# A small add and its place: row sums written to PSUM ahead of a reciprocal, in a kernel of attention and two mixture stages

## The chip, the cores and the metric

The program runs on one core of one Trainium2 chip. The metric is device time of one execution in microseconds (us), as the median of several runs; smaller is better. One further execution was profiled.

## The reference

Attention over 4 batches, 8 heads, 576 positions and 64 dimensions with a causal mask by blocks of 64, then a dense stage of three products with a maximum over them, then a routed stage in which each of 2304 tokens goes to two of eight experts. What bears on the change is the softmax:

```
scores = q @ k.T / sqrt(64), masked where block_i < block_j
scores = scores - max(scores, axis=-1)
attn = exp(scores)
attn = attn / (sum(attn, axis=-1) + 1e-9)
out = attn @ v
```

The outputs of all heads are put side by side into rows of 512, and go on as `x`:

```
h = max(x @ w1, x @ w2, x @ w3);  x = h @ w_out
logits -> top two experts and their weights per token
out[token] += weight * (relu(x @ w1[e]) @ w2[e])
```

## The kernel before, in words

**Jobs.** Attention is cut into 32 jobs of two heads of one batch each. A job is early or late: an early one has the query blocks 0 to 3 (256 rows), a late one the blocks 4 to 8. Jobs 0 to 3 are the early ones of the first batch, jobs 4 to 7 those of the second batch; from job 8 on early and late jobs of the other batches alternate in a written list (`JOBS`). There are 16 late jobs.

**A softmax in one job.** Scores go into a PSUM bank. VectorE takes the negated maximum, ScalarE the exponential with that bias, and the row sum falls out of the same instruction into the small SBUF tile `st`. Then VectorE adds 1e-9 to a few sums in place (128 partitions, 1, 2 or 4 columns), takes the reciprocal in place, and the block of probabilities is multiplied by it, row by row. TensorE then transposes it (against `ident`), an engine copies it from PSUM, and TensorE multiplies it with the values. In an early job the two halves of the scores (blocks 3 and 2, then 0 and 1) have a bank each (`e_scores`, `e_max`, `e_exp`), and there is one add and one reciprocal for all four sums (`e_sums`, lines 352 and 353), then four multiplications (`e_scale`), on VectorE (line 360) or ScalarE (line 362). In a late job the order is block 4, 8, 6, 7, 5; `scale` (lines 366, 367, 371) comes after 8 for 4 and 8, after 7 for 6 and 7, after 5 for 5.

**PSUM.** Scores of kind "s" turn round in two banks; the kind "t", in four banks, takes transposes, value products and all products of the dense stage. Block 8 of a late job has two banks of its own (`a2`). A bank's next user waits for the last instruction that touches its content.

**The opening stage.** The dense weights come as 64-bit words and are taken apart: VectorE shifts (lines 525 and 526), ScalarE converts (line 530), GpSimd adds (line 539); ScalarE and GpSimd then split them into a high and a low part (lines 575 and 573). Meanwhile TensorE does the scores of jobs 0 to 7, the first unit's hidden products (line 584), their maxima being taken by VectorE (line 594), turns and products for the gates (lines 548, 558), and the first unit's long output products (line 601). All of this is handed to a planner (`start`, class `Plan`): each operation has an engine, a cost in us written beside it, the operations it depends on, and the kind of bank that it takes and gives back. The planner runs a clock over these costs and always takes the ready operation with the longest path behind it; instructions are emitted in the order that comes out, and each engine works through its own in that order.

**The rest.** Behind the opening stage the loop over jobs 8 to 31 writes, step by step, the transposes of job j, the scores of job j+1 and a budget of the next unit's dense products (`gap`, `filler`); the framework orders the instructions of this part on each engine by a simulated timeline of its own. For the next late job VectorE and GpSimd prepare low parts of queries, keys and values (lines 278, 272, 287). After the loop come the last unit and the eight experts, with weights split by ScalarE and GpSimd (lines 179, 180).

Of the kernel before, what the change touches and what calls it, by code (L numbers as in the profile page):

```python
# [14 lines left out]
OP = mybir.AluOpType  # L15
# [40 lines left out]
class Plan:  # L56
# [5 lines left out]
    def add(self, engine, cost, emit, deps=(), prio=0.0, take=None, give=None, late=0.1):  # L62
        self.ops.append((engine, cost, emit, tuple(deps), prio, take, give, late))
        return len(self.ops) - 1
# [54 lines left out]
def tile_attention_moe_moe(ctx, tc, qT, kT, v, w1, w2, w3, w_out, gates, noise, e1, e2, out):  # L119
    nc = tc.nc  # L120
# [112 lines left out]
    def bank(kind="m"):  # L233
        n, c = TAGS[kind]
        return (psS if n == "s" else psT).tile([128, 512], F32, name=n, bufs=c)

    psA = []
    RAW, RV, QK, VV, ST, XP = {}, {}, {}, {}, {}, {}
# [51 lines left out]
    def scores(ps, j, i, k0, k1):  # L290
        Kh, Kl = QK[j]
        QH, QL = (x[:, i - 4] for x in QQ)
        nc.tensor.matmul(ps, QH, Kh[:, k0:k1], start=True, stop=False)
        nc.tensor.matmul(ps, QL, Kh[:, k0:k1], start=False, stop=False)
        nc.tensor.matmul(ps, QH, Kl[:, k0:k1], start=False, stop=True)

    def exps(st, c, src, dst):
        ax = AX.XY if len(src.shape) == 3 else AX.X
        nc.vector.tensor_reduce(st[:, 0, c:c + 1], src, axis=ax, op=OP.max, negate=True)
        nc.scalar.activation(dst, src, AF.Exp, bias=st[:, 0, c:c + 1], scale=1.0, accum_out=st[:, 1, c:c + 1])  # L300

    def new_stats(j):
        if j not in ST:
            ST[j] = att.tile([128, 2, 5], F32, name="st", bufs=4)
        return ST[j]

    def s_block(j, i, c):
        st = new_stats(j)
        if i == 8:
            ps = psA[0].tile([128, 2, 512], F32, name="a2")  # L310
            for r in range(2):
                scores(ps[:, r, 0:288], j, i, 288 * r, 288 * r + 288)
            exps(st, c, ps[:, :, 0:288], PL[8][:, :576].rearrange("p (a b) -> p a b", a=2))
            return
        ps = bank("s")[:, :64 * i + 64]
        scores(ps, j, i, 0, 64 * i + 64)
        exps(st, c, ps, PL[i][:, :64 * i + 64])

# [5 lines left out]
    EPS = {}  # L324

    def e_scores(j, h, kind="s"):
        q, k = early_set(j)[:2]
        ps = EPS[j, h] = bank(kind)
        for x, i in zip((0, 256), EB[h]):
            nc.tensor.matmul(ps[:, x:x + 64 * i + 64], q[:, i], k[:, :64 * i + 64], start=True, stop=True)  # L330

    def e_max(j, h):
        st, ps = new_stats(j), EPS[j, h]
        for a, (x, i) in enumerate(zip((0, 256), EB[h])):
            nc.vector.tensor_reduce(ps[:, 448 + a:449 + a], ps[:, x:x + 64 * i + 64], axis=AX.X, op=OP.max, negate=True)
        nc.vector.tensor_scalar(st[:, 0, 2 * h:2 * h + 2], ps[:, 448:450], 0.125, None, op0=OP.mult)

    def e_exp(j, h):
        st, ps, p = ST[j], EPS[j, h], early_set(j)[3]
        for x, i in zip((0, 256), EB[h]):  # L340
            n, c = 64 * i + 64, EC[i]
            nc.scalar.activation(p[:, POFF[i]:POFF[i] + n], ps[:, x:x + n], AF.Exp, bias=st[:, 0, c:c + 1],
                                 scale=0.125, accum_out=st[:, 1, c:c + 1])
# [4 lines left out]
        e_exp(j, h)  # L348

    def e_sums(j):  # L350
        st = ST[j][:, 1, 0:4]
        nc.vector.tensor_scalar(st, st, 1.0e-9, None, op0=OP.add)
        nc.vector.reciprocal(st, st)

    def e_scale(j, on):
        for i, c in EC.items():
            P = early_set(j)[3][:, POFF[i]:POFF[i] + 64 * i + 64]
            x = ST[j][:, 1, c:c + 1]
            if on != "ACT":
                (nc.vector if on == "DVE" else nc.gpsimd).tensor_scalar(P, P, x, None, op0=OP.mult)  # L360
            else:
                nc.scalar.activation(P, P, AF.Copy, scale=x)

    def scale(j, c0, blocks):
        st = ST[j][:, 1, c0:c0 + len(blocks)]
        nc.vector.tensor_scalar(st, st, 1.0e-9, None, op0=OP.add)
        nc.vector.reciprocal(st, st)
        for c, i in enumerate(blocks):
            s = ST[j][:, 1, c0 + c:c0 + c + 1]
            P = PL[i][:, :64 * i + 64]  # L370
            nc.vector.tensor_scalar(P, P, s, None, op0=OP.mult)
# [24 lines left out]
    def e_turn(j, key):  # L396
        p = early_set(j)[3]
        ps = EPS[j, "t", key] = bank("t")
        for a, i in enumerate(range(4) if key == 0 else (2, 3)):
            o = POFF[i] + 128 * key  # L400
            nc.tensor.transpose(ps[:, 128 * a:128 * a + 128], p[:, o:o + 128], ident)

    def e_copy(j, key, eng):
        n = 2 if key else 4
        dst = early_set(j)[4][:, :, 256 * key:256 * key + 64 * n].rearrange("p h (i c) -> p i h c", c=64)
        src = EPS[j, "t", key][:, :128 * n].rearrange("p (i h c) -> p i h c", i=n, h=2)
        if eng == "ACT":
            nc.scalar.activation(dst, src, AF.Copy)
        else:
            nc.vector.tensor_copy(dst, src)  # L410
# [24 lines left out]
    def e_values(j, r):  # L435
        V, _, pt = early_set(j)[2:]
        if r == 0:
            EPS[j] = bank("t")[:, :256]
        p, m = EPS[j], slice(64 * r, 64 * r + 64)
        nc.tensor.matmul(p[m], V[:, r, 0:64], pt[:, r, 0:256], start=True, stop=False)  # L440
        nc.tensor.matmul(p[m, 128:256], V[:, r, 64:128], pt[:, r, 256:384], start=False, stop=True)

    def e_out(j):
        late, b, g = JOBS[j]
        x = new_x(2 * b, g)
        if b == 0:
            nc.scalar.activation(x, EPS[j], AF.Copy)
        else:
            nc.scalar.activation(x[:, 0], EPS[j], AF.Copy)
            nc.vector.tensor_sub(x[:, 1], EPS[j], plain(x[:, 0]))  # L450
# [172 lines left out]
    def start():  # L623
        pl = Plan({"s": 2, "t": 4})
        add = pl.add
# [28 lines left out]
        def job(j):  # L654
            old = next((x for x in range(j) if SETS[x] == SETS[j]), None)
            p = j + 0.5 if j < 4 else 25.0 + j
            sb = "t" if j in (1, 3) else "s"
            ex = []
            for h in (0, 1):
                s = ES[j, h] = add("PE", (0.76, 0.34)[h], lambda h=h: e_scores(j, h, sb), [LQ[j], LV[j]], p, take=sb)  # L660
                m = add("DVE", (0.7, 0.45)[h], lambda h=h: e_max(j, h), [s], p)
                ex.append(add("ACT", (0.9, 0.7)[h], lambda h=h: e_exp(j, h), [m] + ([ET[old]] if old is not None else []),
                              p, give=sb))
            r = add("DVE", 0.2, lambda: e_sums(j), ex, p)
            sc = "ACT" if j in (0, 4, 6) else "DVE"
            c = add(sc, 1.1 if sc == "DVE" else 1.35, lambda: e_scale(j, sc), [r], p)
            cp = []
            for key in (0, 1):
                ET[j] = add("PE", (0.46, 0.25)[key], lambda key=key: e_turn(j, key), [c], p, take="t")
                cp.append(add("ACT", (0.55, 0.4)[key], lambda key=key: e_copy(j, key, "ACT"),  # L670
                              [ET[j]] + ([EV[old]] if old is not None else []), p, give="t"))
            v = add("PE", 0.66, lambda: e_values(j, 0), cp + [LV[j]], p, take="t")
            v = EV[j] = add("PE", 0.66, lambda: e_values(j, 1), [v], p)
            EX[j] = add("ACT", 0.35 if j < 4 else 0.8, lambda: e_out(j), [v], p, give="t")
# [7 lines left out]
        for j in range(4):  # L682
            job(j)
# [45 lines left out]
        for g in range(3):  # L729
            cs = []  # L730
            for c in (0, 1):
                a = add("PE", 0.5, lambda g=g, c=c: gate_turn(g, c), [AD[18 + 2 * g], AD[19 + 2 * g]] + cs, 60.0, take="t")
                cs.append(add("ACT", 0.65, lambda g=g, c=c: gate_copy(g, c), [a] + ([done_g] if done_g else []), 45.0,
                              give="t"))
# [228 lines left out]
    def score_steps(j):  # L963
        if j >= NJ:
            return []
        if LATE[j]:
            return [lambda: s_block(j, 4, 0), lambda: (s_block(j, 8, 1), scale(j, 0, (4, 8))),
                    lambda: s_block(j, 6, 2), lambda: (s_block(j, 7, 3), scale(j, 2, (6, 7))),
                    lambda: (s_block(j, 5, 4), scale(j, 4, (5,)))]
        return [lambda: s_early(j, 0), lambda: (s_early(j, 1), e_sums(j), e_scale(j, "ACT"))]  # L970
# [93 lines left out]
    def bank2():  # L1064
        turn[0] ^= 1
        if turn[0]:
            return ps2.tile([128, 512], F32, name="b")
        return psT.tile([128, 512], F32, name="t", bufs=4)
# [150 lines left out]
    ps = bank2()  # L1219
# [77 lines left out]
    with tc.If(full > 0):  # L1297
# [10 lines left out]
        with tc.For_i(0, E) as e:  # L1308
# [4 lines left out]
            with tc.For_i(0, NT) as t:  # L1313
# [6 lines left out]
                ps = ps3.tile([128, 4, 128], F32, name="pa")  # L1320
# [66 lines left out]
```

## Time and profile before

| | us |
|---|---|
| median of 3 runs | 1029.79 |
| lowest and highest | 1027.38 and 1373.50 |
| the profiled execution | 1033.76 |
| its span from first to last instruction | 1032.0 |
| TensorE busy | 994.0 (96%) |
| VectorE busy | 495.6 (48%) |
| GpSimd busy | 457.2 (44%) |
| ScalarE busy | 418.3 (41%) |

The mean granted clock of TensorE over the span is 0.986 of full speed. In the profile the engines are PE (TensorE), PEld (its weight loads), DVE (VectorE), ACT (ScalarE), POOL (GpSimd) and SP. A row of a timeline gives the start, the time that a merged group of like instructions took, the engine, the line of the kernel, the operation, what it writes and reads, the count, and in brackets the engine's idle time ahead of it with what ended it. A tile is named by what was allocated under that name, so jobs share names: in the opening stage `Ph` holds probabilities of jobs 1, 2, 4 and 5, `Pl` of jobs 3 and 6, `pe` of jobs 0, 7 and 8, and scores stand as `s` or `t`.

### The profile page before, as it was taken

To read this page: it belongs to the slowest core of one execution; us is meant where nothing else is said; L and a number is where in the kernel's file an instruction comes from. 1 tells how busy PE (TensorE), PEld (TensorE's weight loads), DVE (VectorE), ACT (ScalarE), POOL (GpSimd) and SP (SyncE) were. 2 spreads that over 40 slices of the span, in tenths; PEclk is the share of its full clock that TensorE was granted. 3 is DMA by queue.
4 is the path that set the end of the run, shared out by engine and by line. 5 is a ranking of instruction groups with operands and counts; after the bars stand their busy time and mean duration, and the time that the engine had idled before them with its cause. 6 is when DMAs were issued, how large, how long until landed. Compare 5 with 4: busy or idle time off the path is not lost. (4 is left out here: it accounts for less than half of the span.)

```text
span 1032.0 us, 17334 instructions
## 1 busy us (share of the span) xinstructions
PE 994.0 (96%) x6557; PEld 903.8 (88%) x6557; DVE 495.6 (48%) x1328; ACT 418.3 (41%) x997; POOL 457.2 (44%) x381
## 2 busy tenths in 40 slices
PE   8979999999999999998999999999999999999997
PEld 5857899999999998898999979789898989888895
DVE  6883647866688857866237412222222222132221
ACT  5566446655456626545114332323141413242210
POOL 2776131331325232341224478765565648474302
PEclk9988999999999999999999999999999999999999
DMA  8921314312121211111202357563444435342201
GB/s 261 301 89 40 129 33 135 98 51 62 39 62 45 70 35 54 52 51 36 76 22 72 104 186 210 154 199 115 150 145 141 163 102 174 123 144 101 69 12 56
DMA packets 76262, 107.30 MB, mean 104 GB/s; under 512 B 23672, under 2 KB 48248, under 8 KB 76176
## 3 DMA queue, kind: packets, MB, share of 16 engines
q1 hardware_dynamic: 63408, 75.97, 23.9%
q0 software_dynamic: 10592, 29.41, 8.7%
q8 instruction: 52, 0.85, 0.3%
q10 hardware_dynamic: 2176, 0.79, 0.3%
q14 instruction: 34, 0.28, 0.1%
HBM read 86.66 MB, written 20.53 MB: 104 GB/s over the span
## 5 line engine op out<-in xcount | busy, mean ns | idle before, releaser
L180 POOL TENSOR_TENSOR w<-rw,w 128x1536 fp32r<-128x1536 f32 (+1 forms) x45 | 141.2, 3142 | 76.6 <-ACT w L179 62.5
L179 ACT ACTIVATE w<-rw 128x1536 fp32r<-128x1536 f32 (+1 forms) x45 | 60.3, 1343 | 114.5 <-DMA rw<-in_e 62.7
L1117 PE MATMUL b<-xh,w 128*128 128x384 f32 (+7 forms) x272 | 86.9, 321 | 0.9 <-ACT xh L1107 0.9
L1118 PE MATMUL b<-xl,w 128*128 128x384 f32 (+7 forms) x272 | 87.1, 320 | 0.1
L1119 PE MATMUL b<-xh,w 128*128 128x384 f32 (+7 forms) x272 | 87.0, 320 | 0.0
L762 PE MATMUL t<-xB,w 128*128 128x256 f32 x288 | 82.4, 287 | 1.6 <-DVE hm L769 0.9
L762 PE MATMUL t<-xA,w 128*128 128x256 f32 x288 | 82.2, 285 | 1.1 <-DVE hm L769 0.9
L763 PE MATMUL t<-xA,w 128*128 128x256 f32 x288 | 81.8, 284 | 1.0 <-DVE xA L450 1.0
L763 PE MATMUL t<-xB,w 128*128 128x256 f32 x288 | 82.3, 286 | 0.0
L764 PE MATMUL t<-xB,w 128*128 128x256 f32 x288 | 81.9, 285 | 0.0
L764 PE MATMUL t<-xA,w 128*128 128x256 f32 x288 | 81.5, 283 | 0.0
L777 POOL TENSOR_TENSOR hl<-hm,hh 128x512 fp32r<-128x512 f32 x21 | 27.7, 1321 | 114.8 <-ACT hh L776 113.8
L1166 POOL DMA_INDIRECT out_rows<-y,isc x40 | 40.6, 1014 | 79.5 <-DVE y L1165 72.6
L1122 DVE SCALAR_TENSOR_TENSOR ht<-b,ht 128x384 fp32r<-128x384 f32 (+6 forms) x56 | 29.1, 520 | 95.8 <-ACT ht L1121 95.8
L1161 PE MATMUL b<-w,ht 128*128 128x512 f32 (+1 forms) x168 | 67.4, 401 | 2.3 <-ACT ht L1121 2.3
L1165 DVE SCALAR_TENSOR_TENSOR y<-b,idt,prev 128x512 f32<-128x512 f32 (+1 forms) x24 | 18.0, 750 | 104.2 <-PE b L1163 76.3
L1119 PE MATMUL t<-xh,w 128*128 128x256 f32 x240 | 67.4, 281 | 0.0
L1118 PE MATMUL t<-xl,w 128*128 128x256 f32 x240 | 67.3, 281 | 0.0
L1117 PE MATMUL t<-xh,w 128*128 128x256 f32 x240 | 67.0, 281 | 0.0
L1163 PE MATMUL b<-w,ht 128*128 128x512 f32 (+1 forms) x168 | 66.7, 397 | 0.0
L1162 PE MATMUL b<-w,ht 128*128 128x512 f32 (+1 forms) x168 | 66.5, 396 | 0.0
L379 DVE TENSOR_TENSOR Pl<-t,Ph 128x512 fp32r<-128x512 f32 (+2 forms) x96 | 54.3, 572 | 20.3 <-ACT Ph L378 16.6
(388 smaller groups left out, 3019.1 us busy)
## 6 DMA issues: line engine op xcount, KB each, us to landing
rw<-in_e SPq DMA_DIRECT2D x32, 768.0 KB, 4.5
w<-in_w SPq DMA_DIRECT2D x18, 512.0 KB, 7.2
rw<-in_e SPq DMA_DIRECT2D x16, 512.0 KB, 3.7
rv<-in_v SPq DMA_DIRECT2D x16, 320.0 KB, 3.4
rk<-in_kT SPq DMA_DIRECT2D x16, 288.0 KB, 3.0
x2d<-x SPq DMA_DIRECT2D x18, 256.0 KB, 2.0
out_rows<-x SPq DMA_DIRECT2D x9, 512.0 KB, 3.1
w<-in_w_out SPq DMA_DIRECT2D x6, 512.0 KB, 6.7
```

What stands on the lines that cost most here:

```text
L179: nc.scalar.activation(t[:, 0, :c], r[:, :c], AF.Copy)
L180: nc.gpsimd.tensor_sub(t[:, 1, :c], r[:, :c], plain(t[:, 0, :c]))
L379: nc.vector.tensor_sub(dl, src, plain(dh))
L762: nc.tensor.matmul(ps[:, j], wh, x[:, 0], start=kt == 0, stop=False)
L763: nc.tensor.matmul(ps[:, j], wh, x[:, 1], start=False, stop=False)
L764: nc.tensor.matmul(ps[:, j], wl, x[:, 0], start=False, stop=kt == 3)
L1117: nc.tensor.matmul(p, wt1(e, 0, kt, f), th[:, kt, c0:c1], start=kt == 0, stop=False)
L1118: nc.tensor.matmul(p, wt1(e, 0, kt, f), tl[:, kt, c0:c1], start=False, stop=False)
L1119: nc.tensor.matmul(p, wt1(e, 1, kt, f), th[:, kt, c0:c1], start=False, stop=kt == 3)
L1161: nc.tensor.matmul(ps, a, wt2(e, 0, f), start=f == 0, stop=False)
L1162: nc.tensor.matmul(ps, a, wt2(e, 1, f), start=False, stop=False)
L1163: nc.tensor.matmul(ps, l, wt2(e, 0, f), start=False, stop=f == 7)
```

## The change

In `e_sums` and in `scale` the sum plus 1e-9 is no longer written back to `st` in SBUF. It goes into unused columns of a PSUM bank of scores: for an early job the bank of its second half (columns 456 to 459), for a late job the bank of the first block of the group (columns 500 and up of the bank of block 4, 6 or 5). The reciprocal reads it there and writes `st`. In the planner an early job's first half returns its bank after its exponentials, as before; the second half's bank is returned after the sums. The scaling of jobs 5 and 7 moves from VectorE to ScalarE in the opening stage, so that all of jobs 4 to 7 are scaled there.

```
+    SB = {}
 ...
     def s_block(j, i, c):
 ...
-        ps = bank("s")[:, :64 * i + 64]
+        SB[i] = bank("s")
+        ps = SB[i][:, :64 * i + 64]
 ...
     def e_sums(j):
-        st = ST[j][:, 1, 0:4]
-        nc.vector.tensor_scalar(st, st, 1.0e-9, None, op0=OP.add)
-        nc.vector.reciprocal(st, st)
+        st, z = ST[j][:, 1, 0:4], EPS[j, 1][:, 456:460]
+        nc.vector.tensor_scalar(z, st, 1.0e-9, None, op0=OP.add)
+        nc.vector.reciprocal(st, z)
 ...
     def scale(j, c0, blocks):
-        st = ST[j][:, 1, c0:c0 + len(blocks)]
-        nc.vector.tensor_scalar(st, st, 1.0e-9, None, op0=OP.add)
-        nc.vector.reciprocal(st, st)
+        st, z = ST[j][:, 1, c0:c0 + len(blocks)], SB[blocks[0]][:, 500:500 + len(blocks)]
+        nc.vector.tensor_scalar(z, st, 1.0e-9, None, op0=OP.add)
+        nc.vector.reciprocal(st, z)
 ...
     # in the planner, for each early job
-                              p, give=sb))
-            r = add("DVE", 0.2, lambda: e_sums(j), ex, p)
-            sc = "ACT" if j in (0, 4, 6) else "DVE"
+                              p, give=None if h else sb))
+            r = add("DVE", 0.2, lambda: e_sums(j), ex, p, give=sb)
+            sc = "DVE" if j in (1, 2, 3) else "ACT"
             c = add(sc, 1.1 if sc == "DVE" else 1.35, lambda: e_scale(j, sc), [r], p)
```

## Rows read from the trace of the kernel before

**Rows 1.** Busy us by stretch (instructions in brackets), granted clock, DMA share, GB/s.

```profile
core 0: us, PE busy (x) PEld busy (x) DVE busy (x) ACT busy (x) POOL busy (x), PEclk, DMA share, GB/s
52.00:62.00 10.00, 8.49 (x39) 6.72 (x38) 9.12 (x20) 7.58 (x20) 10.00 (x10) 1.00 0.56 204
...
68.70:73.70 5.00, 0.00 (x0) 0.00 (x0) 4.60 (x9) 2.05 (x9) 2.61 (x3) 0.78 0.00 0
73.70:83.10 9.40, 9.37 (x36) 8.72 (x37) 5.40 (x15) 6.59 (x20) 2.78 (x3) 0.50 0.13 31
83.10:97.10 14.00, 13.20 (x87) 10.86 (x86) 5.91 (x20) 11.22 (x33) 7.11 (x6) 0.93 0.15 41
97.10:130.00 32.90, 32.90 (x202) 25.95 (x202) 18.18 (x77) 14.91 (x42) 10.96 (x11) 1.00 0.34 111
130.00:482.00 352.00, 341.26 (x2671) 328.89 (x2669) 254.80 (x718) 194.90 (x528) 107.74 (x116) 1.00 0.20 59
```

**Rows 2.** Timeline of TensorE around the end of the opening stage.

```profile
66.80 1.89 PE L584 MATMUL t<-hl,w 128*128 128x256 f32 x8
73.73 1.22 PE L330 MATMUL s<-kve,qe 128*128 128x64 f32 x4 [5.03 <-ACT Pl L342]
...
97.12 4.45 PE L601 MATMUL t<-xB,hh 128*128 128x512 f32 x10
```

**Rows 3.** Timeline of ScalarE in the same stretch.

```profile
71.65 1.38 ACT L362 ACTIVATE Ph<-Ph,st 128x256 f32<-128x256 f32 x4 [5.37 <-DVE st L353]
72.94 0.29 ACT L342 ACTIVATE Pl<-s,st 128x64 f32<-128x64 f32 x1
...
73.48 0.19 ACT L342 ACTIVATION_READ_ACCUMULATOR Pl<-s,st 128x1 f32 x1
```

**Rows 4.** Timeline of VectorE in the same stretch.

```profile
65.80 5.55 DVE L352 TENSOR_SCALAR st<-st 128x4 f32<-128x4 f32 x1 [0.94 <-ACT Ph L342]
```

**Rows 5.** Timeline of GpSimd in the same stretch and behind it.

```profile
64.01 3.72 POOL L573 TENSOR_TENSOR w<-w 128x512 fp32r<-128x512 f32 x3
67.68 0.62 POOL L229 MEMSET Qh<- 128x640 f32 x1
68.27 2.47 POOL L573 TENSOR_TENSOR w<-w 128x512 fp32r<-128x512 f32 x2
70.69 0.62 POOL L229 MEMSET Ql<- 128x640 f32 x1
80.32 4.04 POOL L573 TENSOR_TENSOR w<-w 128x512 fp32r<-128x512 f32 x3 [9.01 <-ACT w L575]
```

**Rows 6.** Whole run: single lines, ns least/median/most, first and last start.

```profile
L352 DVE TENSOR_SCALAR st<-st x16: 159/172/5547, 11.0 to 275.2; 128x4 f32<-128x4 f32 x16
...
L525 DVE TENSOR_SCALAR sh<-w x24: 674/695/714, 12.8 to 61.2; 128x512 int32<-128x512 int32 x24
...
L336 DVE TENSOR_SCALAR st<-s x28: 97/159/161, 8.0 to 273.2; 128x2 f32<-128x2 f32 x28
```

**Rows 7.** Timeline of VectorE some microseconds later.

```profile
80.03 0.48 DVE L278 SCALAR_TENSOR_TENSOR Ql<-rq,Qh 64x320 fp32r<-64x320 f32 x1
80.44 1.24 DVE L352 TENSOR_SCALAR st<-st 128x4 f32<-128x4 f32 x1
81.71 1.52 DVE L278 SCALAR_TENSOR_TENSOR Ql<-rq,Qh 64x320 fp32r<-64x320 f32 x1
```

**Rows 8.** Line 366 in the whole run: busy us, mean ns, idle time before.

```profile
L366 DVE TENSOR_SCALAR st<-st 128x2 f32<-128x2 f32 (+1 forms) x48 | 12.9, 268 | 4.3 <-ACT p L300 3.5 <-issue 0.3
```

**Rows 9.** Timelines: block 5's scores and line 367, first and last late job.

```profile
107.40 0.34 PE L293 MATMUL s<-Kh,Qh 128*128 128x384 f32 x1
...
111.27 0.17 DVE L367 RECIPROCAL st<-st 128x2 f32<-128x2 f32 x1
...
473.89 0.34 PE L293 MATMUL s<-Kh,Qh 128*128 128x384 f32 x1
...
475.16 0.16 DVE L367 RECIPROCAL st<-st 128x2 f32<-128x2 f32 x1
```

**Rows 10.** What TensorE waited for, 110 to 482 us: total, times, longest.

```profile
PE s L293 <- ACT p L300: 0.7, 1, 0.7
```

## The prediction

> **What bounds the kernel now.** The first view is the busy table by stretch [rows 1]. TensorE works 32.90 of 32.90 us in the stretch from 97.1 us and 341.26 of 352.00 us in the loop over the attention jobs, so there anything spent on VectorE, ScalarE or GpSimd is covered unless TensorE stands in line for it. [...]
>
> [...] TensorE's scores of job 7, second half, start at 73.73 after 5.03 us of waiting for the exponentials of job 6 [rows 2]. Those exponentials run from 72.94 to 73.67, behind job 4's scaling on ScalarE, which waited 5.37 us for VectorE's reciprocal [rows 3]. The reciprocal stands behind the add of 1e-9 to four numbers, which takes 5.55 us, from 65.80 to 71.35 [rows 4]. In that time GpSimd runs without a pause from 64.01 to 71.31 [rows 5]: the add ends when GpSimd has run dry. A tiny add from SBUF to SBUF is thus the head of a chain of four engines.
>
> The third view, all executions of single lines, shows that this is a matter of place and not of work [rows 6]. Line 352 takes 172 ns in the median, 5547 at most. Line 525 is the same operation, but from SBUF into PSUM: 24 times, 674 to 714 ns for 512 columns, never longer, though GpSimd was busy all 10.00 us from 52 to 62 [rows 1] and the last of them started at 61.2. The last view asks what the loop's banks allow; it comes below.
>
> **The change, part by part.** The sum is made against the profiled execution, 1033.76 us (span 1032.0 and 1.76 around it). The median of the runs shown is 1029.79, 3.97 lower; the third run, 1373.50, lies far from the other two and carries nothing here.
>
> *Sums into PSUM, early jobs.* Sixteen adds lose their SBUF output. By line 525 the add no longer waits. Its own price is unseen for 4 columns from SBUF into PSUM; its nearest rows are line 336, which crosses the other way with 2 columns in 159 ns, and line 525, 695 ns for 512 columns [rows 6]; between these ends I take 0.16, by the row with the like number of columns. The reciprocal that reads PSUM is unseen too; line 336 reads PSUM in 159 ns where the SBUF add takes 159 at least and 172 in the median, so I take no change. If the price of both is off by 0.02 us, that is 64 times 0.02 = 1.3 us of VectorE time either way, hidden by VectorE's idle time (254.80 busy of 352.00 in the loop, rows 1).
>
> [...]
>
> In the opening the gain is worked out thus. Undelayed, job 4's sums end at about 66.2, its scaling (1.38 us) at 67.7, job 6's exponentials (0.73 us) at 68.4, and its sums, which the next bank now waits for too, at 68.8. TensorE's last group before the hole ends at 68.69 [rows 2]. Upper bound: the whole 5.03 us, and with no idle time no low clock: the 9.37 us busy at 0.50 are worth 4.7, together 9.7. Lower bound: the low clock stays and ScalarE's added 2.76 us (two scalings of 1.38) fall into the place of the wait, 5.03 - 2.76 = 2.3. I size ScalarE: from 68.7 to 97.1 it is busy 2.05 + 6.59 + 11.22 = 19.9 us [rows 1], the change puts two more scalings of 1.38 on it, 22.6 in 28.4 us. If all of that must be done before TensorE's long products at 97.12, 5.8 us can be saved; if the conversions that ScalarE starts last there can follow later, up to the 9.7. I take 6.5, nearer to ScalarE's bound, because ScalarE is the fuller engine from 83.1 on (11.22 of 14.00). The bounds are 2.3 and 9.7.
>
> The other two stalls of this line in the opening are near 1 us. The one at 80.44 has a neighbour, line 278, with two SBUF inputs, that stalls as well [rows 7]; it stays. I count them at nothing, but if the order shifts they are up to 1 us each.
>
> [...] The add at 80.44 took 1.24 us and line 278 behind it 1.52, against 0.48 a moment before, while GpSimd was in a run of three instructions of 4.04 us [rows 5, 7], about one instruction each; the one at 65.80 waited through six. [...]
>
> *Scales of jobs 5 and 7 to ScalarE.* VectorE loses two groups of four, ScalarE gains 2.8 us, counted above. Nothing on VectorE that needs SBUF at both ends is then left near the hole to inherit its stall.
>
> *Banks held longer, early.* The second half's bank comes back after the reciprocal instead of after the exponential: the add and the reciprocal, about 0.35 us, plus VectorE's queue. Scores of job 5, second half, wait for job 4's sums, 66.2 instead of 65.82. That is inside the 6.5. The planner lays the stage out afresh with the new returns and costs, so neighbours may swap in any queue; the longest group that could slip ahead of the scores is line 584's of 1.89 us [rows 2], and it is inside the bounds too.
>
> *Late jobs.* 48 adds go into the first block's score bank. They carry 12.9 us where 48 times 0.159 would be 7.6, so 5.3 us of stall [rows 8], for which no instruction of TensorE waited; behind them stands the scaling, SBUF at both ends, which will wait in their place. Gain: nothing. But two new waits arise in each of the 16 late jobs. Two banks turn round for blocks 4, 6, 7, 5 (block 8 has its own). Block 7 reuses block 4's bank, which now is busy until the reciprocal for blocks 4 and 8; block 5 reuses block 6's, busy until the reciprocal for 6 and 7, and that lies behind block 7's exponential. In the first late job block 5's scores start at 107.40 and that reciprocal ends at 111.44, 4.0 us later; in the last 473.89 and 475.33, 1.4 later [rows 9]. Of the 32 places 16 start today before the release they would have to wait for, by 55 us together. Behind such a wait stands all of TensorE's queue. What covers it is that the order outside the planned stage is laid out by a simulated timeline, which puts other ready products first; the unit products fill the loop. Bounds: 0 and +55. I take +2, near the lower end, because today's bank waits of the same kind cost 0.7 us in the whole loop [rows 10] with the same ordering. If that cover fails, block 5's max, exponential and scaling, about 3 us, become the next late thing.
>
> Sum: 1033.76 - 6.5 + 2 = 1029.3 for an execution like the profiled one, and 1029.79 - 4.5 = **1025.3** for the median.
>
> **The rivals.** *Full gain:* ScalarE's extra work finds room, the clock stays up, the loop costs nothing: -9.7, about 1020. For it: ScalarE was idle 2.95 of 5.00 us in the hole. Against: 11.22 of 14.00 later. Chance 0.20.
>
> *The held bank decides (the slower side):* TensorE stands at block 5's scores (line 293) because the laid-out order expects the reciprocal earlier than it comes. Above 6.5 us in sum, 0.4 us for each of 16 jobs, the change is slower than before; a third of the 55 us gives +12, about 1042; half gives +21, about 1051. For it: lags of 1 to 8 us at half of the places. Against: rows 10. Chance 0.20, of which 0.07 above 2%.
>
> *The change does not do what it says:* the add still waits when its output is in PSUM, since its input stays in SBUF. Then 1030 to 1033, the early scores with the longer-held banks. Against it stands line 525, from SBUF as well. Chance 0.06.
>
> *Forecast,* saving 1 to 8 us: 0.50. The remaining 0.04 is for more than 2% saved, which would need a second hole to close (TensorE's idle time in the loop is 10.7 us).
>
> **How the numbers follow.** 2% is 20.6 us, about what a measurement of this kernel can tell from no change. Faster by that: 0.04. Slower: 0.07. Within: 0.89. The range reaches from beyond the full gain, with the 3 us by which runs shown differ, 1014, to the held bank at a quarter of its price, +14 against 6.5, 1038.
>
> **What would show it.** In the changed profile: the early add (line 352 before) at 0.16 to 0.2 us everywhere; no hole of 5 us near 69 us and a granted clock of 1.00 there; TensorE's first long product (line 601 before) some 6 us earlier than 97.12; ScalarE fuller before it. In the loop, waits of the late scores' matmuls (line 293 before) for VectorE's reciprocal, in sum 0 to 4 us. Wrong would be: a new hole in the opening with ScalarE at its end, or waits at block 5's scores above 6 us in sum.

## The result and the profile after

| kernel | median us | least to most | runs | ratio to before, 95% interval |
|---|---|---|---|---|
| before | 1028.74 | 1024.87 to 1373.5 | 12 | |
| after | 1035.98 | 1032.01 to 1040.4 | 12 | 1.0076 [1.0055, 1.0097] |

The change makes the kernel slower by 0.76%, some 8 us (the run of 1373.5 us, far above the others, is left out of the ratio). Forecast were 1025.3 us, a gain of 4.5; the time is inside the range and inside 2%, but on the other side. The prediction took 2% as about what can be told from no change; the interval here is 0.2% to either side, so the loss is clear. Lines behind 317 stand three lower in the new kernel: 352 became 355, 353 became 356, 366 and 367 became 369 and 370, 371 became 374.

The opening looks as the prediction said. First the busy table by stretch of the changed kernel, with the columns of [rows 1]:

```profile
core 0: us, PE busy (x) PEld busy (x) DVE busy (x) ACT busy (x) POOL busy (x), PEclk, DMA share, GB/s
68.70:73.70 5.00, 5.00 (x38) 4.76 (x38) 2.56 (x10) 4.95 (x18) 2.38 (x3) 1.00 0.29 68
73.70:83.10 9.40, 9.14 (x63) 6.99 (x62) 2.36 (x9) 9.04 (x28) 1.66 (x2) 1.00 0.16 41
83.10:97.10 14.00, 12.86 (x48) 8.33 (x46) 1.80 (x5) 7.92 (x20) 14.00 (x13) 0.76 0.19 54
```

TensorE now works 5.00 of 5.00 us where it stood still [rows 1], at a granted clock of 1.00. The low clock has moved rather than gone, though: 0.76 in the row from 83.10, where the trace has 6.8 us at 0.50 from 86.0 us on, behind a wait of 1.14 us. The timeline of the same kernel around that place (start, us, engine, line, operation, tiles) and all its executions of the early add (ns least, median, most; first and last start):

```profile
65.75 0.17 DVE L355 TENSOR_SCALAR s<-st 128x4 f32<-128x4 f32 x1 [0.93 <-ACT Ph L345]
67.23 1.89 PE L587 MATMUL t<-hl,w 128*128 128x256 f32 x8
68.96 0.61 PE L333 MATMUL s<-kve,qe 128*128 128x64 f32 x4
...
88.94 6.37 PE L604 MATMUL t<-xB,hh 128*128 128x512 f32 x10
```

```profile
L355 DVE TENSOR_SCALAR s<-st x14: 153/166/167, 10.3 to 274.3; 128x4 f32<-128x4 f32 x14
...
L355 DVE TENSOR_SCALAR t<-st x2: 151/153/155, 16.6 to 20.1; 128x4 f32<-128x4 f32 x2
```

The add that took 5.55 us [rows 4] takes 0.17, the most of all sixteen is 167 ns, job 7's scores follow the group before them without a gap, and the first long product starts at 88.94 where it started at 97.12 [rows 2]: 8.2 us earlier. And yet the last product of this execution starts 3.3 us later than in the one before the change (1027.9 against 1024.6). So 8 us are won at 90 us, and 11 are lost behind it. Two questions follow: was there a hole in the other executions of the kernel before, and what is lost behind the opening? The waits of TensorE in the changed kernel from 110 to 560 us (engine, tile, line, what it waited for: us in total, times, longest) begin:

```profile
PE t L377 <- DVE p L374: 3.4, 2, 3.2
PE t L377 <- DVE Pl L382: 2.4, 1, 2.4
PE t L443 <- ACT rt L877: 2.3, 1, 2.3
PE s L293 <- ACT p L300: 1.5, 3, 0.6
PE s L294 <- DVE Ql L278: 1.4, 1, 1.4
```

The wait that the prediction named, scores (line 293) for the late reciprocal (line 370), is not among them. The long waits are few: transposes of a late block for its scaling (line 374), early value products (line 443).

### The profile page after: what moved, and what is told of

The parts are those of the page before. It is cut to its first block, busy times and chain, and to the rows that moved or that the text cites. A ratio compares the mean times of both kernels' runs of the same rounds, so it can differ in the third digit from the quotient of the medians.

```text
span 1035.2 us, 17369 instructions
## 1 busy us (share of the span) xinstructions
PE 995.3 (96%) x6557; PEld 902.8 (87%) x6557; DVE 482.7 (47%) x1320; ACT 424.1 (41%) x1005; POOL 455.8 (44%) x381
## 5 line engine op out<-in xcount | busy, mean ns | idle before, releaser
L765 PE MATMUL t<-xA,w 128*128 128x256 f32 x288 | 83.3, 289 | 1.0 <-DVE hm L772 0.9
L766 PE MATMUL t<-xA,w 128*128 128x256 f32 x288 | 82.5, 286 | 0.0
L767 PE MATMUL t<-xA,w 128*128 128x256 f32 x288 | 82.4, 286 | 0.0
L272 POOL TENSOR_TENSOR Kl<-rk,Kh 128x576 fp32r<-128x576 f32 x16 | 23.3, 1458 | 100.4 <-ACT Kh L271 100.4
```

Of the source, the lines that this page charges most:

```text
L765: nc.tensor.matmul(ps[:, j], wh, x[:, 0], start=kt == 0, stop=False)
L766: nc.tensor.matmul(ps[:, j], wh, x[:, 1], start=False, stop=False)
L767: nc.tensor.matmul(ps[:, j], wl, x[:, 0], start=False, stop=kt == 3)
```

## The experiments

The theories in the expectations: **H**, the banks held until the reciprocal cost the time; **W**, arithmetic on PSUM itself costs it; **P**, the lines happen to be laid out in a worse order, without relation to banks; **U**, the hole near 70 us belongs to the one profiled execution, against **S**, it is in every one; **R**, chance. All ratios are to the kernel before on the same chip, as recorded; the quotient of two medians can differ from them by up to 0.2%.

### Each half alone

Early sums in PSUM, late ones as before:

```diff
-        st, z = ST[j][:, 1, c0:c0 + len(blocks)], SB[blocks[0]][:, 500:500 + len(blocks)]
-        nc.vector.tensor_scalar(z, st, 1.0e-9, None, op0=OP.add)
-        nc.vector.reciprocal(st, z)
+        st = ST[j][:, 1, c0:c0 + len(blocks)]
+        nc.vector.tensor_scalar(st, st, 1.0e-9, None, op0=OP.add)
+        nc.vector.reciprocal(st, st)
```

> The change without its late half: early sums in PSUM, scales of jobs 5 and 7 on ScalarE, the late jobs' add in place in SBUF as before. Theory H (the longer-held score banks of the late jobs cost the time): the opening's gain of 7.2 us (long products at 88.9 in place of 97.1) is kept to the end, ratio to before 0.992 to 0.996. Theory W (the add and the reciprocal through PSUM cost more by themselves): about the same as H here, a little less gain. Theory P (any edit makes the framework lay the loop out anew, and this layout happened to be worse): ratio anywhere from 0.99 to 1.01, without relation to the opening's gain.

Measured: 1028.22 us, ratio 0.9993 [0.9976, 1.0011]. The reverse, the kernel before with the late sums alone in the score banks (the `SB` lines and `scale` of the diff):

> The late half alone: late sums in the bank of the group's first block, everything of the early jobs as before. H: slower than before by 10 to 15 us, ratio 1.010 to 1.015, with the hole of 5 us at 69 us still there and the loss in the loop from 110 to 490 us. W: also slower. P: anywhere from 0.99 to 1.01.

Measured: 1030.83 us, 1.0024 [1.0008, 1.0040]. Neither half is the whole: -0.07% and +0.24% don't add up to +0.76%. The early half, for which the sum had 6.5 us, brings none that can be told from nothing. In us: -0.7 and +2.5 make +1.8, and both together cost 7.8, so 6 us (some 3 to either side, by the three intervals) appear only when both halves are there. The expectation for the late half, 10 to 15 us with the hole still there, missed in both: in its profile there is no hole, and the early add in SBUF at that place reads:

```profile
65.61 0.52 DVE L355 TENSOR_SCALAR st<-st 128x4 f32<-128x4 f32 x1 [0.94 <-ACT Ph L345]
```

### The late sums in another bank

The whole change, but the sums of blocks 4, 8, 6 and 7 go to spare columns of block 8's own two banks, which don't turn round with the score banks; block 5's go to block 5's bank.

```diff
-            ps = psA[0].tile([128, 2, 512], F32, name="a2")
+            ps = SB[8] = psA[0].tile([128, 2, 512], F32, name="a2")
...
-        st, z = ST[j][:, 1, c0:c0 + len(blocks)], SB[blocks[0]][:, 500:500 + len(blocks)]
+        st, z = ST[j][:, 1, c0:c0 + len(blocks)], (SB[5] if blocks[0] == 5 else SB[8][:, 0])[:, 500 - c0:500 - c0 + len(blocks)]
```

> The whole change, but the late sums of blocks 4 and 8 and of 6 and 7 go into spare columns of block 8's own banks, so that the two score banks come back after the exponentials as in the kernel before; block 5's sum stays in its bank. H: as fast as the early half alone, ratio 0.992 to 0.997. W (PSUM itself): as slow as the whole change, 1.005 to 1.010. P: anywhere from 0.99 to 1.01.

Measured: 1026.26 us, 0.9981 [0.9966, 0.9997]. The same arithmetic on PSUM, with the sums of blocks 4, 8, 6 and 7 in another bank, is not slow: W falls.

### A hold without the arithmetic, first try

The kernel with the early half alone, and a write into the score bank behind the late reciprocal:

```diff
+        nc.vector.memset(SB[blocks[0]][:, 500:501], 0.0)
```

> Early half as changed; the late add and reciprocal in SBUF as before, but a memset of one column in the bank of the group's first block follows the reciprocal, so the bank is held as long as in the change while no sum goes through PSUM. The 48 memsets cost some 0.1 us each on VectorE, off TensorE's path. H: as slow as the whole change, ratio 1.005 to 1.012. W: as fast as the early half alone, 0.992 to 0.997. P: anywhere from 0.99 to 1.01.

Measured: 1028.61 us, 1.0006 [0.9991, 1.0021]. This tested nothing: the write uses nothing that the reciprocal makes, and in the trace it ran ahead of it (at 163.5 us with the reciprocal at 165.7, at 242.1 with 246.9), so the bank was not held as long as in the change.

### Both kernels profiled again

No edit: the kernel before and the changed one, once more.

> The kernel before, unchanged, profiled once more. Theory U (the stall of 5.55 us and the hole of 5.03 us at 69 us belonged to the one profiled execution, which at 1033.76 us was 5 us above the median): here the add at 66 us takes under 2 us, TensorE has no hole near 69 us, the first long product starts near 89.5 as in the run with the late half alone, not at 97.1, and the span is 1026 to 1028. Theory S (the hole is in every execution, and something later gives its gain back): stall of 5 us and hole again, first long product near 97.

> The changed kernel, unchanged, profiled once more. Theory P (the order that the framework lays out for the loop of this kernel costs the time): the same waits of TensorE come back, 2.3 us at 177 behind the second product of an early job, 2.4 us at 411, 1.4 us at 424, and the low clock behind most of them; span 1031 to 1037. Rival R (chance of the one execution): other waits, or the same with less low clock, and a span near 1029.

The kernel before took 1025.41 us (span 1023.6), the changed one 1033.97 (span 1032.2). In the second execution of the kernel before, the busy table (columns as above) and the timeline show at the place of the hole:

```profile
68.70:73.70 5.00, 5.00 (x37) 4.55 (x36) 4.62 (x15) 4.83 (x19) 2.70 (x3) 1.00 0.23 57
73.70:83.10 9.40, 6.65 (x43) 4.98 (x42) 6.53 (x15) 6.38 (x20) 3.75 (x3) 1.00 0.18 46
```

```profile
66.08 0.52 DVE L352 TENSOR_SCALAR st<-st 128x4 f32<-128x4 f32 x1 [0.93 <-ACT Ph L342]
...
68.98 0.71 PE L330 MATMUL s<-kve,qe 128*128 128x64 f32 x4
...
64.08 3.72 POOL L573 TENSOR_TENSOR w<-w 128x512 fp32r<-128x512 f32 x3
67.74 0.63 POOL L229 MEMSET Qh<- 128x640 f32 x1
68.33 2.50 POOL L573 TENSOR_TENSOR w<-w 128x512 fp32r<-128x512 f32 x2
...
89.96 4.45 PE L601 MATMUL t<-xB,hh 128*128 128x512 f32 x10
```

The same add, beside the same GpSimd instructions at the same times within 0.3 us [rows 4, 5], takes 0.52 us and not 5.55; there is no hole of 5 us (the 2.75 us of idle time from 73.70 on are waits of 1.1 us or less), and the first long product starts at 89.96, not at 97.12. The kernel with the late half alone, whose early jobs are those of the kernel before, agrees (0.52 us, 89.51). U stands, S falls: one execution of three has the hole. That one, at 1033.76 us, lies above 87 of the 89 timed runs of the kernel before (the others are 1034.33 and 1373.5): it was no typical one, and its time alone was a hint.

The changed kernel's second execution has the long waits of its first again (2.60 us at 171, 2.43 at 405, 1.39 at 419, 3.22 at 482), so R falls. Against the second execution of the kernel before it shows where the loss is. A unit product is here a matmul of line 762 (765 in the changed kernel), the first of three lines with a unit's hidden products, 576 in all. First starts, us:

| | before, again | after, again |
|---|---|---|
| first long product | 89.96 | 87.48 |
| unit product 1 of 576 | 109.4 | 105.5 |
| unit product 83 | 180.8 | 180.6 |
| unit product 329 | 369.5 | 370.4 |
| unit product 370 | 418.3 | 423.4 |
| unit product 452 | 488.3 | 495.0 |
| unit product 576 | 542.5 | 549.1 |
| last expert product | 1015.8 | 1024.4 |

By the first unit product 3.9 us are won; 3.7 of them are lost again by 181 us, 1.1 more by 370, 4.2 between 370 and 423, 1.6 by 490 and 2.0 in the experts. But not all of the 3.9 is gain: the changed order has 509 matmuls ahead of the first unit product, the kernel before 520. The 11 others are scores and come behind it: unit products are drawn forward. The kernel with the late half alone has the same 509, and the early half alone has 520 and starts its first unit product at 110.0.

### Two tries at chance

The changed kernel with a write into the score bank behind the late reciprocal (this time it did follow it, since the bank's own sums are read there), and the changed kernel with the scales of jobs 5 and 7 on VectorE as before:

```diff
-        nc.vector.reciprocal(st, z)
+        nc.vector.reciprocal(st, z); nc.vector.memset(SB[blocks[0]][:, 504:505], 0.0)
```

```diff
-            sc = "DVE" if j in (1, 2, 3) else "ACT"
+            sc = "ACT" if j in (0, 4, 6) else "DVE"
```

> The whole change plus a memset of one unused column of the same bank behind each late reciprocal, some 0.1 us on VectorE 48 times, and the banks held that much longer. It does more work than the change everywhere and holds longer. Theory H (held banks) and theory W (PSUM itself): ratio to before 1.007 to 1.012, no better than the change. Theory P (the laid-out order): the memsets shift the simulated timeline, another order comes out, and the ratio lies with the other variants, 0.997 to 1.004.

> The whole change, but the scales of jobs 5 and 7 stay on VectorE. On TensorE its order differs from the change's in some places of the opening stage only; the loop's order is the same. Theory P: as slow as the change, 1.005 to 1.010, with the same waits at 177, 411 and 424 us. If the loss sits in the opening (two more scales on ScalarE, 1.4 us each): 0.998 to 1.004.

Measured: 1034.34 us, 1.0054 [1.0036, 1.0072], and 1034.73 us, 1.0070 [1.0050, 1.0089]. Both keep most of the loss, and both show the long waits of the changed kernel again (2.90 and 2.56 us at line 443 near 175 us, 3.96 and 3.23 at line 377 near 485). The first has the changed kernel's matmul (by tiles and shape) at 6221 of 6557 places in TensorE's order, so it says little against P; the second moves the scales of the opening alone, so the loss is not theirs.

### What held banks do, seen in the two traces

The two places with a long wait lie at the end of a unit's dense products, the work that fills TensorE between the jobs' steps. Timeline of the kernel before, again: last of those products (line 788), scores of block 6 (448 columns) and of block 5 (384), the reciprocal (367) and scaling (371) of the late sums, and the wait behind:

```profile
162.76 0.45 PE L293 MATMUL s<-Kh,Qh 128*128 128x448 f32 x1
165.87 0.29 PE L788 MATMUL t<-w,hl 128*128 128x264 f32 x1
172.93 0.83 PE L440 MATMUL t<-pte,kve 128*64 128x256 f32 x3 [0.24 <-DVE pte L410]
...
466.83 0.34 PE L293 MATMUL s<-Kh,Qh 128*128 128x384 f32 x1
468.11 0.16 DVE L367 RECIPROCAL st<-st 128x2 f32<-128x2 f32 x1
468.94 0.29 PE L788 MATMUL t<-w,hl 128*128 128x264 f32 x1
469.95 0.42 DVE L371 TENSOR_SCALAR p<-p,st 128x384 f32<-128x384 f32 x1
476.20 0.55 PE L374 MATMUL t<-ident,p 128*128 128x128 f32 x3 [2.61 <-DVE Pl L379]
```

And of the changed kernel, again (those products: line 791):

```profile
162.58 0.29 PE L791 MATMUL t<-w,hl 128*128 128x264 f32 x1
163.56 0.18 DVE L356 RECIPROCAL st<-s 128x4 f32<-128x4 f32 x1
166.07 0.45 PE L293 MATMUL s<-Kh,Qh 128*128 128x448 f32 x1
170.89 1.08 PE L443 MATMUL t<-pte,kve 128*64 128x256 f32 x2 [2.60 <-ACT rt L877]
...
473.74 0.28 PE L791 MATMUL t<-w,hl 128*128 128x264 f32 x1
474.71 0.17 DVE L370 RECIPROCAL st<-s 128x2 f32<-128x2 f32 x1
476.72 0.42 PE L293 MATMUL s<-Kh,Qh 128*128 128x384 f32 x1
481.58 0.41 DVE L374 TENSOR_SCALAR p<-p,st 128x384 f32<-128x384 f32 x1
482.14 0.87 PE L377 MATMUL t<-ident,p 128*128 128x128 f32 x3 [3.22 <-DVE p L374]
```

Read the last late job. Before, block 5's scores start 1.3 us ahead of the reciprocal for blocks 6 and 7, and 1.9 us of dense products still follow to cover block 5's softmax. After, they come 1.8 us behind that reciprocal, when the dense products are used up, and max, exponential and scaling of block 5 stand bare: 3.22 us, where 2.61 were paid before. At 163 us the same happens to block 6: before, its scores start 3.4 us ahead of the end of the last dense product (162.76 against 166.16), after, 3.2 behind it and 2.3 behind the early job's reciprocal, and the wait behind grows from 0.24 to 2.60.

Which bank is waited for is not quite what the prediction had. Another late job of the changed kernel, again, shows it:

```profile
317.48 0.69 ACT L300 ACTIVATE p<-s,st 128x512 f32<-128x512 f32 x1 [1.07 <-DVE st L299]
318.31 0.44 PE L293 MATMUL s<-Kh,Qh 128*128 128x384 f32 x1 [0.62 <-ACT p L300]
318.98 0.16 DVE L370 RECIPROCAL st<-s 128x2 f32<-128x2 f32 x1
```

Block 5's scores start here 0.14 us behind the end of block 7's exponential and ahead of the reciprocal for 6 and 7. Over the 16 late jobs of this trace they are ahead of that reciprocal in 5, and never ahead of block 7's exponential; in the kernel before, again, they are ahead of block 7's exponential in 11, and never ahead of block 6's. So block 5 does not wait for block 6's held bank: going by these starts, it gets block 7's instead, and its wait is for block 7's exponential. Block 7 does wait for block 4's held bank: behind the reciprocal for 4 and 8 in all 16 jobs, by 0.06 us at the least, where 5 were ahead of it before. The two banks are thus not handed out in strict turn.

Beside such waits stand stretches at the low clock; the busy table of the changed kernel, again, in three such stretches (columns as above):

```profile
170.80:174.20 3.40, 3.31 (x13) 2.58 (x14) 3.21 (x9) 1.87 (x5) 0.19 (x1) 0.50 0.96 295
406.30:413.10 6.80, 6.53 (x23) 5.89 (x23) 4.34 (x19) 1.27 (x4) 0.00 (x0) 0.50 0.00 0
481.40:488.20 6.80, 5.33 (x23) 4.99 (x23) 3.30 (x18) 0.49 (x1) 0.00 (x0) 0.50 0.15 39
```

From 110 to 560 us the stretches at 0.50 sum to 20.5 us there and to 10.2 in the kernel before, again; TensorE is idle for 14.7 against 12.3 us (in the two first executions: 17.1 and 3.4 us at 0.50, 15.6 and 12.7 idle). From the first to the last unit product the changed kernel takes 443.6 us and the kernel before 433.1. Of these 10.5 us, 3.5 are idle time (14.4 against 10.9) and an estimated 4.9 are half of the 9.7 us more that TensorE works at 0.50 (the four products of job 7's scores took 1.22 us at 0.50 [rows 1, 2], and 0.61 in the changed kernel at 1.00); most of the remaining 2.1 is the 11 matmuls that stood ahead of the first unit product before (1.5 us: with the time at 0.50 taken by half, TensorE is busy for 99.5 us ahead of it there and for 98.0 here).

### The true hold, and each hold alone

The kernel with the early half alone, late sums in SBUF, and a copy of the late reciprocals into the score bank, so that the bank is held until they are done, with no arithmetic on it:

```diff
-        nc.vector.reciprocal(st, st)
+        nc.vector.reciprocal(st, st); nc.vector.tensor_copy(SB[blocks[0]][:, 500:500 + len(blocks)], st)
```

> The whole change but with the late sums added and inverted in SBUF as before; after each late reciprocal VectorE copies its result (one to two values a partition, 0.06 to 0.2 us a piece) into a spare column of the score bank in which the change would have put the sums, so the bank is held until after the reciprocal without any arithmetic on it; the output is unchanged. Theory H (the held score banks of the late jobs, together with the early jobs' second banks, cost the time): slower than the kernel before, ratio 1.004 to 1.010, with the first unit product as early as in the changed kernel and a wait of TensorE of 2 us or more near 170 to 180 us. Theory W (the arithmetic on PSUM costs it) and theory P (the order that the lines happen to give): ratio 0.998 to 1.003, as with the early pairs alone.

Measured: 1034.4 us, 1.0043 [1.0026, 1.0060]. Holds without arithmetic in the late jobs bring more than half of the loss back, and the picture with it. TensorE's timeline of this kernel:

```profile
164.34 0.29 PE L791 MATMUL t<-w,hl 128*128 128x264 f32 x1
167.43 0.45 PE L293 MATMUL s<-Kh,Qh 128*128 128x448 f32 x1
169.89 0.50 PE L293 MATMUL s<-Kh,Qh 128*128 128x512 f32 x1 [0.28 <-DVE s L370]
173.95 1.08 PE L443 MATMUL t<-pte,kve 128*64 128x256 f32 x2 [3.09 <-issue]
...
478.73 0.42 PE L293 MATMUL s<-Kh,Qh 128*128 128x384 f32 x1
484.83 0.87 PE L377 MATMUL t<-ident,p 128*128 128x128 f32 x3 [4.02 <-DVE ex L909]
```

Here even the wait that the prediction named shows once, for 0.28 us, though for block 7 (512 columns). The copies add 7.7 us to VectorE over the run. The kernel at 1.0054, with 2.8 us of such writes, lost no more than the change, which speaks against the copies as the loss; they were not run without a hold.

Then the whole change with only blocks 4 and 8, or only 6 and 7, moved to block 8's banks (with the `SB[8]` line above):

```diff
+        ... (SB[8][:, 0] if blocks[0] == 4 else SB[blocks[0]])[:, 500 - c0:500 - c0 + len(blocks)]
```

> The whole change, but the sums of blocks 4 and 8 go to spare columns of block 8's own two banks; those of blocks 6 and 7 stay in block 6's score bank, as in the change. Theory H: if the bank of block 4, held across block 8's exponentials, is the one that costs, ratio 0.997 to 1.001; if it is the bank of block 6, 1.005 to 1.009; if each costs a part, 1.001 to 1.005. Theory P: anything between 0.998 and 1.008 without relation to the other kernel of this pair.

```diff
+        ... (SB[8][:, 0] if blocks[0] == 6 else SB[blocks[0]])[:, 500 - c0:500 - c0 + len(blocks)]
```

> The mirror of the kernel before it: the sums of blocks 6 and 7 go to spare columns of block 8's own two banks, those of blocks 4 and 8 stay in block 4's score bank, as in the change. Theory H: if the bank of block 6, held across block 7's exponentials, is the one that costs, ratio 0.997 to 1.001; if it is the bank of block 4, 1.005 to 1.009; if each costs a part, 1.001 to 1.005, and the two parts add to the 0.8 to 1.0% between the whole change and the kernel with both moved away.

Measured: 1028.79 us, 0.9999 [0.9984, 1.0015], with block 6's bank held; 1025.36 us, 0.9973 [0.9954, 0.9992], with block 4's held. And the whole change with the early pairs of the loop (jobs from 8 on) in SBUF:

```diff
-        st, z = ST[j][:, 1, 0:4], EPS[j, 1][:, 456:460]
+        st = ST[j][:, 1, 0:4]; z = EPS[j, 1][:, 456:460] if j < 8 else st
```

> The whole change, but the early pairs of the jobs from 8 on (those in the loop behind the opening) add and invert in SBUF as before; the early pairs of the opening and all late pairs stay in PSUM. Theory H in its joint form (early and late holds together cost the loop): the early holds of the loop are gone, and with them most of the loss: ratio 0.999 to 1.004, no wait of TensorE over 1.5 us near 170 to 180 us. If the late holds alone cost it, or theory P: ratio 1.005 to 1.009, as the whole change.

Measured: 1029.72 us, 1.0013 [0.9997, 1.0029]. So any one of three holds taken away (block 4's, block 6's, the loop's early one) takes most of the loss away: the joint form of H. The mirror's expectation that the two late parts add up fell: from 0.9981 with both moved, block 6's hold adds 0.18%, block 4's takes 0.08% off (less than the intervals can tell), both together add 0.95%.

The fastest of all kernels is the one with block 4's bank held and blocks 6 and 7 moved. Its timeline:

```profile
165.22 0.29 PE L791 MATMUL t<-w,hl 128*128 128x264 f32 x1
165.34 0.37 PE L293 MATMUL s<-Kh,Qh 128*128 128x448 f32 x1
...
472.09 0.55 PE L377 MATMUL t<-ident,p 128*128 128x128 f32 x3 [1.70 <-DVE Pl L382]
```

Block 6 comes 0.2 us before the dense products' end, and the wait near 480 us is 1.70. Over the kernels, the distance of the first scores of block 6 (first place) and of block 5 (second place) from the end of the last dense product, in us (minus: ahead of it), and TensorE's longest wait there, from one execution each:

| | ratio | first place | longest wait | second place | longest wait |
|---|---|---|---|---|---|
| before, again | 1 | -3.4 | 1.03 | -2.4 | 2.61 |
| early alone | 0.9993 | -3.1 | 1.31 | -2.4 | 2.61 |
| 6, 7 moved | 0.9973 | -0.2 | 0.79 | -1.8 | 1.70 |
| all moved | 0.9981 | -0.2 | 0.44 | -2.4 | 1.65 |
| first try at a hold | 1.0006 | -0.2 | 0.66 | -2.0 | 2.04 |
| loop's early in SBUF | 1.0013 | +0.4 | 1.41 | +2.7 | 3.23 |
| late alone | 1.0024 | +0.4 | 1.21 | +2.7 | 3.22 |
| 4, 8 moved | 0.9999 | +2.9 | 2.47 | -0.2 | 2.75 |
| true hold | 1.0043 | +2.8 | 3.09 | +2.8 | 4.02 |
| write behind the reciprocal | 1.0054 | +2.8 | 2.90 | +2.8 | 3.96 |
| scales back | 1.0070 | +2.9 | 2.56 | +2.7 | 3.23 |
| after, again | 1.0076 | +3.2 | 2.60 | +2.7 | 3.22 |

Kernels that are late by over 2 us at one of the places lose 0 to 0.24%; the four late at both lose 0.43 to 0.76%. The table also says which holds make a place late: the first needs the loop's early hold together with block 6's (4, 8 moved), the second block 4's together with block 6's (late alone). Only the kernels with all three are late at both, which is why taking any one away helps so much; P, an order without relation to the banks, does not fit this. What it costs does not add up from the two places, though. The largest step in the table of starts, 4.2 us between 370 and 423, lies at neither: there TensorE idles 2.3 us longer, 1.39 of it at 419 us for a low part that VectorE prepares (line 278), with 3.4 us at 0.50 behind that wait. Of the four kernels only the changed one and the one with the scales back have this wait (0.76 and 0.70%); the other two lose 0.43 and 0.54%.

## Why the prediction was wrong

**The sum.** Forecast was -4.5 us (-6.5 in the opening, +2 for the late jobs), measured +7.8. Of the 12.3 us between, 5.8 are the opening's term (-0.7 with the early half alone), 0.5 the late jobs' (+2.5 alone), and 6 had no term: they appear only when the early and the late banks are held together. The signs that were named for being right came (the short add, no hole, the first long product earlier, no waits at line 293 for the reciprocal), and neither sign of being wrong did; they looked at the places where the mechanism was expected, and the loss was elsewhere.

**What bounds the kernel.** Right for the loop: TensorE is the bound (busy for 437.7 of the 450 us from 110 to 560 in the kernel before, again), and a softmax step costs only where nothing covers it. Wrong for the opening: the hole was read from one execution, and that one was dearer than the others.

**Sums into PSUM, early jobs: the first step that failed.** Right that the add no longer waits, wrong in what that is worth. All sixteen adds take 151 to 167 ns, as sized (0.16), and the hole is gone; the first long product is 8.2 us earlier against the execution shown, where some 6 were forecast. But in two other executions with the early adds in SBUF the add took 0.52 us, with the first long product at 89.96 and 89.51; over the eleven executions with early sums in PSUM it starts at 87.42 to 90.22. The early half alone ran at 0.9993, -0.7 us in an interval from -2.5 to +1.1. The prediction noted that the execution lay 3.97 us above the median, took the same 4.5 off the median as off the execution, and did not ask whether the hole was that difference. By the adds of those two executions, 0.52 against 0.16, the step is worth an estimated 0.4 us at that place, which the interval takes in. The low clock did not go for good either: nine of those eleven executions have 3.4 to 6.8 us at 0.50 between 85 and 105 us, the two others without the hole none.

**No surcharge for PSUM.** Right. All executions of the late sums' lines (busy us, mean ns | idle before), in the kernel before, again, and then in the changed one:

```profile
L366 DVE TENSOR_SCALAR st<-st 128x2 f32<-128x2 f32 (+1 forms) x48 | 12.9, 268 | 4.4 <-ACT p L300 3.8
L367 DVE RECIPROCAL st<-st 128x2 f32<-128x2 f32 (+1 forms) x48 | 7.8, 163 | 1.1
```

```profile
L370 DVE RECIPROCAL st<-s 128x2 f32<-128x2 f32 (+1 forms) x48 | 8.0, 166 | 1.2
L369 DVE TENSOR_SCALAR s<-st 128x2 f32<-128x2 f32 (+1 forms) x48 | 7.7, 161 | 13.7 <-ACT p L300 13.1 <-issue 0.2
```

The reciprocal reads PSUM in 166 ns and SBUF in 163. The two sources differ by 3 ns here, an estimated 0.1 us over the 48. The add lost the 5.2 us of stall that [rows 8] showed, 12.9 to 7.7, and the scaling behind it did not inherit it (37.1 us of busy time before, again, and 37.6 after), against what the prediction said; no TensorE instruction had waited for it, so it gained nothing, as said. New is the idle time: VectorE now stands 13.7 us instead of 4.4 in front of these adds, nearly all of it for ScalarE's exponential; why the laid-out order puts them so early was not tried.

**Late jobs.** By themselves they cost what was taken: +2.5 us in an interval from 0.8 to 4.1, against +2. The way is another. +2 was taken, near the lower end, because "a simulated timeline, which puts other ready products first" covers the waits. The cover is real: no wait for the late reciprocal is named in the changed kernel. But it was counted as free, and it is a stock: putting dense products first uses them up, and at a unit's end the later softmax steps have none left. The prediction named that next late thing, "block 5's max, exponential and scaling, about 3 us"; the last late job pays 3.22, but it had paid 2.61 before. "Block 5 reuses block 6's" held before the change and not behind it, where block 5 follows block 7's exponential. The rival of the held bank was right in cause (the true hold, 1.0043; the sums in another bank, 0.9981); wrong in its place, line 293, and its price, a third of 55 us, is twice the 8.5 that late and joint holds cost together.

**Banks held longer, early: the second step that failed.** The hold of the early second halves was priced in the opening alone, and the late holds as if it were not there. Eight of the sixteen early jobs run in the loop, where their bank delays the next late job's block. The late holds without these eight cost 0.13% (in an interval that takes in nothing), with them 0.76%: this is the term of 6 us that the sum lacks.

**Scales on ScalarE.** No cost: 1.0070 with them back, 1.0076 without, the intervals overlap.

**Left open.** The holds change the order in which the framework lays the instructions out, and that order was never changed without the holds, nor kept with them; so it is shown that the three holds together cost the time, and argued from single executions that they do it by drawing dense products forward. Why the places don't add up is open. The 2.0 us lost in the experts were not tried. What makes the add wait 5.55 us in one execution and 0.52 in others was not either.

## What to carry to other kernels

Before a hole in one profiled execution is priced, hold that execution's time against the other runs, and look at a second execution: a hole of 5 us in a run that lies 5 us above the rest is probably that run's. A scalar parked in a buffer that turns round holds the buffer for longer. Any two of the three holds cost at most 0.24% here and all three 0.43 to 0.76%, so holds are to be priced together, over every place where they occur. The price showed where the work that covered them ran out, not at the instruction that waits for the buffer; a bank outside the turn held most of the late scalars at no cost (0.9981). Count covering work as a stock, by unit and not on average.

## What the runs showed of the hardware

- The same VectorE add from SBUF to SBUF, 4 columns, beside the same GpSimd instructions: 5.55 us in one execution, 0.52 in the next. In the kernel with the late half alone it took 0.52 as well, and a later one, at 69.30, took 1.67; the most in the second execution of the kernel before was 1.67 too. The 0.52 is shorter than one of the GpSimd instructions beside it (1.24 us, 3.72 / 3); the 5.55 spans six.
- With the output in PSUM and the input still in SBUF the add never waited: 151 to 167 ns in 16 executions, though GpSimd was at work beside several of them (the one at 65.75, 0.17 us, lies inside a GpSimd group of 3.73 us from 63.74 on).
- Waits of TensorE of 2.4 to 3.2 us stand beside stretches of 3.4 to 6.8 us at a granted clock of 0.50 in the changed kernel, again: with 2.4 us more of idle time than in the kernel before, again, such stretches grew from 10.2 to 20.5 us between 110 and 560 us; half of the difference, an estimated 5.1 us, is about twice what the idle time costs. It is no fixed pairing: a wait of 2.60 us at 403 us in the kernel with blocks 6 and 7 moved has no such stretch beside it (granted clock 1.00 from 400 to 430).
